# Regrouping the attention work inside the steps of a fused attention and feed-forward kernel, with exp(phi) one step sooner and q's transpose called at the front of its step

## The chip, the cores and the metric

The kernel runs on one core of one Trainium2 chip. The metric is the device time of one execution in microseconds (us). A profile's span, from its first to its last instruction, is about 1.8 us shorter than the time of the same execution.

## The reference, cut to what matters

Each of 8 batches pools k and v with weights made from phi, attends from q to the 32 pooled memories of each of 8 heads, and the result x goes through a normalised two-layer feed-forward with a residual:

```python
a = np.exp(phi - max); a = a / (np.sum(a, axis=2, keepdims=True) + 1e-09)
k_m = np.einsum('bhsm,bhsd->bhmd', a, k)
v_m = np.einsum('bhsm,bhsd->bhmd', a, v)
attn = softmax(scale * np.matmul(q, k_m.transpose(0, 1, 3, 2)))
x = np.matmul(attn, v_m)                       # then heads side by side: 8 x 576 x 512
xn = (x - mu) / np.sqrt(var + 1e-06) * g_ln
out = x + np.maximum(xn @ w_ch1, 0.0) @ w_ch2  # 512 -> 2048 -> 512
```

## The kernel before

The kernel works in steps, one for each batch b. A step has the first product of b (`mm1`, PSUM tiles h_ps), then the second product (`mm2`, ch_ps), four tiles of 128 rows in an even step and five in an odd one. Between the half tiles of the second product, 8 matmuls each, stands the attention work of the next batch, nb = b + 1, in the slots `ex[0]`, `ex[1]` and so on. Pooling is `a_kv`, the sums of the pooling weights `a_sum`, the transposes of the pooled k and v `a_tr`, the scores `a_sc`, the softmax's denominators `a_den` (which ends in Eh, the normalised weights), the first product's weights with v folded in `a_w1b`, and x and its statistics `x_tiles`.

```python
    for b in range(1, B):
        mm1(b, 0, JC)
        ...
        if b > 1:
            x_rstd(pr, tiles[0:2])
        if nb < B:
            ex[0] += [lambda: a_exp(nb), lambda: a_qT(nb, 0), lambda: a_kv(nb)]
            if nb + 1 < B:
                ex[0] += [lambda: phis.update({nb + 1: load_phi(nb + 1)})]
            ex[1] += [lambda: a_tr(nb)]
        ...
        ex[1] += [lambda: x_tiles(pr, t1)]
        if nb < B:
            ex[2] += [lambda: a_sum(nb), lambda: a_w1b(nb, 0), lambda: a_w1b(nb, 1)]
            ex[3] += [lambda: a_sc(nb)]
            ex[3] += [lambda: a_vb(nb)]
            ex[4] += [lambda: a_den(nb)]
            ex[5] += [lambda: a_w1b(nb, 2), lambda: a_w1b(nb, 3)]
            ex[6] += [lambda: x_tiles(nb // 2, [4, 5] if nb % 2 else [0, 1])]
            if nb + 1 < B:
                ex[7] += [lambda: load(nb + 1)]
```

`load` puts k, v and q of a batch into GpSimd's queue, which converts them to bf16 on the way; the pre-summation of exp(phi) for the sums (es) stands in the same queue, in program order. The transposed q comes from a DMA that the sync queue issues:

```python
    def a_qT(b, i):
        ...
                nc.sync.dma_start_transpose(out=s["qT"].rearrange("p j n x -> p (j n) x"),
                                            in_=s["q"].rearrange("p j n x -> p (j n x)"))
```

And nearly all PSUM tiles of the attention work rotate through one set of three buffers (`tag="big", bufs=3`).

The softmax here doesn't subtract the row's maximum and nothing guards it: scores larger than these inputs give would overflow.

## Time and profile before

| | before |
|---|---|
| time, median of 4 runs | 262.76 us |
| span of the profiled run | 261.1 us |
| TensorE busy | 245.4 us, 94% |
| granted TensorE clock, mean | 0.993 |
| second product, odd step (batch 3) | 22.63 us |
| second product, even step (batch 2) | 18.25 us |

The prediction below shows the lines that carry this. These are rows of the timeline of before in batch 2: start, length of the issue, instruction.

```profile
93.36 3.15 SPq L287 DMA_TRANSPOSE qT<-q_bf  x1
...
104.57 0.79 POOL L84 DMA_DIRECT2D kv_bf<-in_k_dram  x1
...
105.36 0.76 POOL L84 DMA_DIRECT2D kv_bf<-in_v_dram  x1
...
106.34 0.77 POOL L92 DMA_DIRECT2D q_bf<-in_q_dram  x1
...
107.93 0.47 PE L310 MATMUL sc_ps<-qT,kvT 64*32 64x320 bf16 x16
```

The transposing DMA of q is issued early in the first product, and lands 5.0 us later by the trace's list of DMA issues (median of six). The loads for the batch after next go out 11 us after it, when it is long done. They have to wait that long because GpSimd first works on es, and es waits for exp(phi), which stands behind the first product on ScalarE. Nobody wrote this order down as a rule: it is a by-product of where exp(phi) stands.

### The profile page before, as it was taken

The numbers are of one execution on the slowest core, as the hardware profiler recorded it, in microseconds if no ns is written. First come the engines' busy times: TensorE is split into PE (matmuls) and PEld (weight loads), VectorE is DVE, ScalarE is ACT, GpSimd is POOL, SyncE is SP. The second block draws the span as 40 slices with busy tenths as digits, with TensorE's granted clock in tenths as the row PEclk, the third lists the DMA queues.
The fourth block names the chain that finished last, engine by engine and source line by source line (L and its number), as shares of the span: only waits on it lengthen the run. The fifth ranks groups of instructions, "written<-read, shape, count | busy, mean of one in ns | idle before, by whom it ended". The sixth has DMA issues, their size and how long they took to land.

```text
span 261.1 us, 5808 instructions
## 1 busy us (share of the span) xinstructions
PE 245.4 (94%) x2453; PEld 132.2 (51%) x2453; DVE 154.9 (59%) x307; ACT 127.9 (49%) x218; POOL 51.9 (20%) x87
## 2 busy tenths in 40 slices
PE   7868996989989999999999999999999999999994
PEld 3434642437533475447543574457443664466453
DVE  3346716576485943876385754695477637684431
ACT  3165643356545185448546283647345472566210
POOL 8633230000440005400440007100710014000000
PEclk9999998999999999999999999999999999999999
DMA  7999999965689193895589391988499451121133
GB/s 159 195 207 207 206 253 251 244 138 102 134 118 234 43 182 92 153 233 114 128 143 210 81 199 56 189 186 120 137 182 189 90 94 43 44 55 25 43 80 80
DMA packets 41922, 36.82 MB, mean 141 GB/s; under 512 B 17444, under 2 KB 37160, under 8 KB 41896
## 3 DMA queue, kind: packets, MB, share of 16 engines
q0 software_dynamic: 17248, 19.53, 43.8%
q1 hardware_dynamic: 24488, 16.79, 28.0%
q8 instruction: 19, 0.31, 0.4%
q10 hardware_dynamic: 160, 0.13, 0.2%
q14 instruction: 7, 0.06, 0.1%
HBM read 41.42 MB, written 9.44 MB: 195 GB/s over the span
## 4 chain that ended last, share of the span: by engine, by line
PE 64%; DMA 18%; DVE 10%; ACT 4%; POOL 2%; issue 1%; SPq 0%; POOLq 0%
PE ch_ps L438 33%; PE h_ps L374 21%; DMA phi_st<-in_phi_dram 7%; DMA out_dram<-x_sb 6%; DMA w1r<-in_moe_w_ch_dram 4%; DVE w1b L357 3%; DVE bst L416 3%; PE kv_ps L205 2%; PE o_ps L404 2%; DVE Eh L339 2%; ACT x_sb L410 2%; PE w1b_ps L353 1%; PE last_ps L450 1%; DVE x_sb L462 1%; POOL kv_bf L84 1%
## 5 line engine op out<-in xcount | busy, mean ns | idle before, releaser
L438 PE MATMUL ch_ps<-w2b,rT 128*128 128x512 bf16 x560 | 131.8, 382 | 2.2 <-DVE x_sb L462 2.2
L438 PEld LDWEIGHTS <-rT 128*128 128x128 bf16 x560 | 51.2, 98 | 64.5 <-issue 9.6
L380 ACT ACTIVATE rT<-h_ps 128x576 bf16<-128x576 f32 x88 | 52.6, 649 | 33.0 <-PE h_ps L374 32.9
L374 PE MATMUL h_ps<-Eh,w1b 128*128 128x288 bf16 x512 | 67.3, 285 | 1.5 <-DVE w1b L357 0.8
L374 PEld LDWEIGHTS <-w1b 128*128 128x128 bf16 x512 | 49.5, 97 | 18.8 <-issue 2.7
L382 DVE TENSOR_SCALAR rT<-h_ps 128x576 bf16<-128x576 f32 x40 | 30.3, 756 | 26.9 <-PE h_ps L374 26.9
L357 DVE SCALAR_TENSOR_TENSOR w1b<-m_sb,rsum,w1b_ps 128x512 bf16<-128x512 f32 x64 | 43.6, 739 | 2.9 <-ACT m_sb L169 2.9
L189 POOL TENSOR_TENSOR es<-e_sb 128x512 f32<-128x512 bf16 x6 | 6.9, 1148 | 144.1 <-ACT e_sb L182 144.1
L462 DVE SCALAR_TENSOR_TENSOR x_sb<-ch_ps,rstd,x_sb 128x512 f32<-128x512 f32 x35 | 25.9, 742 | 13.2 <-PE ch_ps L438 12.6
L410 ACT ACTIVATE x_sb<-o_ps 128x1024 f32<-128x1024 f32 (+1 forms) x20 | 18.6, 937 | 29.5 <-PE o_ps L404 28.2
L416 DVE BATCH_NORM_STATS2 bst<-x_sb 128x6 f32<-128x512 f32 x36 | 24.4, 677 | 11.8 <-ACT x_sb L410 11.8
L339 DVE SCALAR_TENSOR_TENSOR Eh<-E_sb,rs,rden 128x576 bf16<-128x576 bf16 x16 | 12.4, 815 | 15.1 <-ACT rden L338 15.1
L315 ACT ACTIVATE E_sb<-sc_ps,rs 128x640 bf16<-128x640 f32 x16 | 11.9, 791 | 13.3 <-PE sc_ps L310 13.3
L424 ACT ACTIVATE rstd<-mv,eps_sb 128x2 f32<-128x2 f32 (+1 forms) x20 | 5.9, 296 | 20.3 <-DVE mv L417 20.3
L353 PE MATMUL w1b_ps<-w1r,kvT 64*32 64x512 bf16 x256 | 11.4, 383 | 1.3 <-DVE w1b L357 0.5
L182 ACT ACTIVATE e_sb<-phi_st 128x1152 bf16<-128x1152 f32 x8 | 9.2, 1153 | 6.2 <-DMA phi_st<-in_phi_dram 6.2
L227 DVE CAST v<-kv_ps 128x128 bf16<-128x128 f32 x8 | 2.3, 292 | 14.6 <-ACT k L220 13.7
L329 ACT ACTIVATE rden<-den_ps 128x576 f32<-128x576 f32 x16 | 9.5, 644 | 2.9 <-PE den_ps L327 2.9
L174 PE MATMUL w_ps<-fill 128*128 128x512 f32 x14 | 9.2, 774 | 1.6 <-DVE fill L119 1.6
L338 ACT ACTIVATE rden<-rden 128x576 f32<-128x576 f32 x16 | 10.0, 682 | 0.0
L404 PE MATMUL o_ps<-vb,Eh 64*128 64x128 bf16 (+1 forms) x160 | 8.5, 221 | 0.9 <-DVE Eh L339 0.9
L205 PEld LDWEIGHTS <-e_sb 64*32 64x32 bf16 x648 | 6.4, 94 | 5.4 <-ACT e_sb L182 3.0
(69 smaller groups left out, 143.4 us busy)
## 6 DMA issues: line engine op xcount, KB each, us to landing
out_dram<-x_sb SPq DMA_DIRECT2D x70, 128.0 KB, 2.4
kv_bf<-in_k_dram POOLq DMA_DIRECT2D x7, 576.0 KB, 6.4
kv_bf<-in_v_dram POOLq DMA_DIRECT2D x7, 576.0 KB, 9.1
phi_st<-in_phi_dram SPq DMA_DIRECT2D x6, 576.0 KB, 4.6
q_bf<-in_q_dram POOLq DMA_DIRECT2D x6, 576.0 KB, 11.7
w1r<-in_moe_w_ch_dram POOLq DMA_DIRECT2D x4, 512.0 KB, 14.2
w2b<-in_moe_w_ch_dram POOLq DMA_DIRECT2D x4, 512.0 KB, 19.3
q_bf<-in_q_dram POOLq DMA_DIRECT2D x4, 288.0 KB, 11.9
```

The lines of the kernel that those rows point to most:

```text
L315: nc.scalar.activation(out=E_[:, g].rearrange("p (a x) -> p a x", a=2), in_=sc[:, :, 0:HP], func=AF.Exp, scale=s["rs"][:, g:g + 1])
L339: nc.vector.scalar_tensor_tensor(out=Eh[:, g, :], in0=s["E"][:, g, 0:S], scalar=s["rs"][:, g:g + 1], in1=rd[:, g].rearrange("p a x -> p (a ...
L353: nc.tensor.matmul(ps[32 * j:32 * (j + 1), g, :], s["kvT"][r:r + 64, 2, 32 * j:32 * (j + 1)], w1r[r:r + 64, j, fs], start=True, stop=True, ...
L357: nc.vector.scalar_tensor_tensor(out=s["w1b"][:, g, fs], in0=m_sb[:, fs], scalar=s["rsum"][:, g:g + 1], in1=ps[:, g, :], op0=ALU.mult, op1 ...
L374: nc.tensor.matmul(h_ps[:, half, 0:HS], s["w1b"][:, g, P * j:P * (j + 1)], s["Eh"][:, g, HS * half:HS * (half + 1)], start=(g == 0), stop= ...
L380: nc.scalar.activation(out=dst, in_=h_ps[:, :, 0:HS], func=AF.Relu)
L382: nc.vector.tensor_scalar(out=dst, in0=h_ps[:, :, 0:HS], scalar1=0.0, scalar2=None, op0=ALU.max)
L404: nc.tensor.matmul(ov.rearrange("p (j e d) -> p j e d", e=2, d=D)[:, :, g, :], s["Eh"][r:r + 64, g, a:z], s["vb"][r:r + 64, g, 2 * u:2 * ( ...
L410: nc.scalar.activation(out=x[:, 0:n].rearrange("p i (u y) -> p i u y", u=2), in_=o_ps.rearrange("p u (i y) -> p i u y", i=2)[:, 0:n], func ...
L416: nc.vector.bn_stats(out=stt, in_=x[:, i, :])
L438: nc.tensor.matmul(ch_ps, rT[:, j, P * t:P * (t + 1)], w2b[:, j, :], start=(j == 0), stop=(j == JC - 1))
L462: nc.vector.scalar_tensor_tensor(out=x, in0=ch_ps, scalar=rstd, in1=x, op0=ALU.mult, op1=ALU.add)
```

## The change

Its intent is to enter and leave the small tiled matmuls less often. Pooling, sums, x of all four full tiles and the transposes become one group after the first half tile; the scores follow one half tile later, all of w1b comes behind den. To have it all ready, exp(phi) moves to the end of the step before, and the call of q's transpose to the front of the step. The loads move in program order too, from `ex[7]` to `ex[2]`. The core of the diff, cuts marked:

```diff
     def a_kv(b):
         ...
+        else:
+            a_sum(b, ps)                # sums into kv's own PSUM tile
         k_out(b, ps, True)
         v_out(b, ps[:, :, D:2 * D])
 ...
-    a_exp(1)
     x_tiles(0, [0, 1])
     x_tiles(0, [2, 3])
 ...
     x_rstd(0, [2, 3])
+    a_exp(1)
 ...
     load(2)
+    a_exp(2)
     for b in range(1, B):
+        if nb < B:
+            a_qT(nb, 0)
         mm1(b, 0, JC)
 ...
-            ex[0] += [lambda: a_exp(nb), lambda: a_qT(nb, 0), lambda: a_kv(nb)]
 ...
+            ex[0] += [lambda: a_kv(nb)]
 ...
+        ex[0] += [lambda: x_tiles(pr, t0, False), lambda: x_tiles(pr, t1, False)]
+            ex[0] += [lambda: a_tr(nb)]
 ...
+        ex[0] += [lambda: x_stats(pr, t0), lambda: x_rstd(pr, t0)]
+            ex[1] += [lambda: a_sc(nb)]
 ...
+        ex[1] += [lambda: x_stats(pr, t1), lambda: x_rstd(pr, t1)]
 ...
+            ex[3] += [lambda: x_tiles(pr, t2), lambda: x_rstd(pr, t2)]     # odd steps
 ...
+            ex[3] += [lambda: a_den(nb)]
+            ex[4] += [lambda: a_w1b(nb, 0), lambda: a_w1b(nb, 1), lambda: a_vb(nb)]
             ex[5] += [lambda: a_w1b(nb, 2), lambda: a_w1b(nb, 3)]
 ...
-                ex[7] += [lambda: load(nb + 1)]
 ...
+            ex[1] += [lambda: phis.update({nb + 1: load_phi(nb + 1)})]
+            ex[2] += [lambda: load(nb + 1)]
+            ex[6] += [lambda: a_exp(nb + 1)]
```

More of the change, by code (lines that the diff above doesn't have):

```diff
@@ L233, in rs_out, with a_sum @@
         st8[b]["rs"] = rs
+    def a_sum(b, ps):
+        for i in range(2):
+            nc.tensor.matmul(ps[:, 0, P:P + 2], st8[b]["es"][:, i, :], ones8,
+                             start=(i == 0), stop=(i == 1))
+        rs_out(b, ps)
     def a_kv(b):
@@ L263, in a_tr @@
             s["rsum"] = rsum
-    def a_sum(b):
-        ps = big([P, 2, 512], FP32, "sum_ps")
-        for i in range(2):
-            nc.tensor.matmul(ps[:, 0, P:P + 2], st8[b]["es"][:, i, :], ones8,
-                             start=(i == 0), stop=(i == 1))
-        rs_out(b, ps)
     def a_vb(b):
@@ L296, in a_qT @@
         dst = s["qT"][:, 2 * i:2 * i + 2].rearrange("p a n x -> p a (n x)")
-        if i == 0:
+        if i == 0 or b == 1:
             nc.scalar.activation(out=dst, in_=q_ps[:, :, 0:NP * P], func=AF.Copy)
@@ L385, with x_tiles @@
     xs = {}
-    def x_tiles(pr, ts):
+    def x_tiles(pr, ts, stats=True):
         n = len(ts)
@@ L412, in x_tiles, with x_stats @@
                              func=AF.Copy)
+        for i, t in enumerate(ts):
+            xs[(pr, t)] = (x, i)
+        if stats:
+            x_stats(pr, ts)
+    def x_stats(pr, ts):
+        x, n = xs[(pr, ts[0])][0], len(ts)
         mv = moe.tile([P, 2, 2], FP32, name="mv", bufs=4)
@@ L536 @@
     a_qT(1, 0)
+    a_w1b(1, 0)
     mm2(0, 2, 8, 12)
     a_qT(1, 1)
-    a_w1b(1, 0)
+    a_w1b(1, 1)
     mm2(0, 2, 12, 16)
     a_sc(1)
-    a_w1b(1, 1)
     mm2(0, 3, 0, 4)
     a_den(1)
-    a_vb(1)
     a_w1b(1, 2)
@@ L548 @@
     a_w1b(1, 3)
+    a_vb(1)
     mm2(0, 3, 8, 16)
     load(2)
+    a_exp(2)
     for b in range(1, B):
         pr = b // 2
-        mm1(b, 0, JC)
+        nb = b + 1
         odd = b % 2
         tiles = [4, 5, 6, 7, 8] if odd else [0, 1, 2, 3]
-        t1, t2 = tiles[2:4], tiles[4:5]
-        nb = b + 1
-        if b > 1:
-            x_rstd(pr, tiles[0:2])
+        t0, t1, t2 = tiles[0:2], tiles[2:4], tiles[4:5]
+        if nb < B:
+            a_qT(nb, 0)
+        mm1(b, 0, JC)
         ex = {i: [] for i in range(2 * len(tiles))}
         if nb < B:
-            ex[0] += [lambda: a_exp(nb), lambda: a_qT(nb, 0), lambda: a_kv(nb)]
-            if nb + 1 < B:
-                ex[0] += [lambda: phis.update({nb + 1: load_phi(nb + 1)})]
-            ex[1] += [lambda: a_tr(nb)]
-        if b == 1:
-            ex[0] += [lambda: x_tiles(0, [4, 5]), lambda: x_rstd(0, [4, 5])]
-        ex[1] += [lambda: x_tiles(pr, t1)]
+            ex[0] += [lambda: a_kv(nb)]
+        ex[0] += [lambda: x_tiles(pr, t0, False), lambda: x_tiles(pr, t1, False)]
         if nb < B:
-            ex[2] += [lambda: a_sum(nb), lambda: a_w1b(nb, 0), lambda: a_w1b(nb, 1)]
-        ex[2] += [lambda: x_rstd(pr, t1)]
+            ex[0] += [lambda: a_tr(nb)]
+        ex[0] += [lambda: x_stats(pr, t0), lambda: x_rstd(pr, t0)]
         if nb < B:
-            ex[3] += [lambda: a_sc(nb)]
+            ex[1] += [lambda: a_sc(nb)]
+        ex[1] += [lambda: x_stats(pr, t1), lambda: x_rstd(pr, t1)]
         if odd:
-            ex[4] += [lambda: x_tiles(pr, t2), lambda: x_rstd(pr, t2)]
+            ex[3] += [lambda: x_tiles(pr, t2), lambda: x_rstd(pr, t2)]
         if nb < B:
-            ex[3] += [lambda: a_vb(nb)]
-            ex[4] += [lambda: a_den(nb)]
+            ex[3] += [lambda: a_den(nb)]
+            ex[4] += [lambda: a_w1b(nb, 0), lambda: a_w1b(nb, 1), lambda: a_vb(nb)]
             ex[5] += [lambda: a_w1b(nb, 2), lambda: a_w1b(nb, 3)]
-            ex[6] += [lambda: x_tiles(nb // 2, [4, 5] if nb % 2 else [0, 1])]
-            if nb + 1 < B:
-                ex[7] += [lambda: load(nb + 1)]
+        if nb + 1 < B:
+            ex[1] += [lambda: phis.update({nb + 1: load_phi(nb + 1)})]
+            ex[2] += [lambda: load(nb + 1)]
+            ex[6] += [lambda: a_exp(nb + 1)]
         for i, t in enumerate(tiles):
```

## The prediction

> **What bounds the kernel now.** I read the page first, then the chain of waits in order of time, then the timelines of the prologue and of one pair of batch steps.
>
> ```profile
> span 261.1 us, 5808 instructions
> PE 245.4 (94%) x2453; PEld 132.2 (51%) x2453; DVE 154.9 (59%) x307; ACT 127.9 (49%) x218; POOL 51.9 (20%) x87
> PE   7868996989989999999999999999999999999994
> ```
>
> TensorE is the bound: from slice 16 to 39 every slice is at 90% or more, and no other engine is above 59%. So only three things move the end: matmul work on TensorE, the cost of changing between kinds of matmul, and stalls of TensorE. The chain of waits shows one even step (four tiles), columns being start, length, what:
>
> ```profile
> 98.87 1.73 PE ch_ps L438 x8
> 100.62 0.80 PE kv_ps L205 x72
> 101.42 1.83 PE ch_ps L438 x8
> ...
> 112.44 0.56 PE w1b_ps L353 x16
> 113.00 1.83 PE ch_ps L438 x8
> 114.83 0.46 PE o_ps L404 x12
> ```
>
> Eight matmuls of the second product take 1.73 us after full-array work and 1.83 after the 64-row attention matmuls: leaving a tiled group costs 0.10. Entering costs about as much: x of one pair of full tiles is four slots of 0.053 but takes 0.33. An inserted tiled group therefore costs about 0.22 beyond its work. By the stretches' table an even step's second product is 18.25 us (98.87 to 117.12) and an odd one's 22.63 (125.26 to 147.89), against 8 x 1.73 = 13.84 and 10 x 1.73 = 17.30; the first product adds 7.95 to 8.14. An even step has almost no stall. An odd one has about 0.8: the second product of batch 3, where the lines are start, length, instruction, and in brackets idle time and its releaser:
>
> ```profile
> 138.88 1.17 ACT L329 ACTIVATE rden<-den_ps 128x576 f32<-128x576 f32 x2
> 139.57 0.11 PEld L353 LDWEIGHTS <-kvT 64*32 64x32 bf16 x7 [0.37 <-issue]
> 140.66 1.55 DVE L339 SCALAR_TENSOR_TENSOR Eh<-E_sb,rs,rden 128x576 bf16<-128x576 bf16 x2 [2.25 <-ACT rden L338]
> 142.79 2.71 DVE L357 SCALAR_TENSOR_TENSOR w1b<-m_sb,rsum,w1b_ps 128x512 bf16<-128x512 f32 x4
> ```
>
> The second w1b group sat 0.3 us until Ln freed its PSUM buffer (three buffers rotate); and its evictions, 0.68 each, run only after both Eh operations, because VectorE keeps program order. The third place is the prologue:
>
> ```profile
> 37.14 1.16 ACT L182 ACTIVATE e_sb<-phi_st 128x1152 bf16<-128x1152 f32 x1 [3.58 <-DMA phi_st<-in_phi_dram]
> 38.21 1.92 ACT L410 ACTIVATE x_sb<-o_ps 128x1024 f32<-128x1024 f32 x2
> 43.24 1.87 PE L438 MATMUL ch_ps<-w2b,rT 128*128 128x512 bf16 x4 [2.21 <-DVE x_sb L462]
> 46.56 0.17 DVE L232 RECIPROCAL rs<-kv_ps 128x2 f32<-128x2 f32 x1 [2.72 <-PE kv_ps L213]
> 46.77 0.38 ACT L220 ACTIVATE k<-kv_ps 128x256 bf16<-128x256 f32 x1 [3.67 <-DVE rs L232]
> 47.18 0.29 DVE L227 CAST v<-kv_ps 128x128 bf16<-128x128 f32 x1 [0.45 <-ACT k L220]
> ```
>
> exp(phi 1) blocks ScalarE until phi has landed, so the x copies are late, and TensorE stands 2.21 us. The last three lines: reciprocal, k and v read one PSUM tile one after another.
>
> **What the Trainium skill says.** "TensorEngine Tiling (Array Packing)", Key Properties: changing the tiling mode drains TensorE. The 1.83 against 1.73 agrees. "PSUM — Partial Sum Buffer", Terms: two engines may not be on one bank at once, reads included. The trace agrees in effect: k waits for rs and v for k. "Perfetto Trace Analysis", Tensor Engine Instruction: ScalarE and VectorE are strict FIFO; Eh before w1b above agrees. "DMA: Bandwidth & Descriptors", Issuing engines are not separate DMA queues: transfers of all queues interleave on the same 16 engines; the prologue's outputs will slow its loads.
>
> **The change part by part.** No arithmetic goes away except that sums no longer take a PSUM tile of their own; nearly everything is moved.
>
> *Prologue.* exp(phi 1) goes behind the rstd pair. The x copies can then start at the end of x, about 33.9, instead of 38.21; statistics end near 38.3, rstd near 38.8, exp(phi 1) near 40.0. The 2.21 us stall goes, and pooling could start at about 41.8 instead of 45.0. But v of batch 1 is issued at 23.08 and takes 19.5 to landing: 42.6. And two outputs of 128 KB now leave before that; at the 206 GB/s shown there they take some 1.3 us of the loads. I put pooling at 43.7, a gain of 1.4. Afterwards the order to the first product of batch 1 is much as before (Eh about 10.3 us after pooling starts, w1b evictions behind it, the first product waiting for them). The two qT copies, 1.24 us on ScalarE each, overlap mm2. **-1.4 us.**
>
> *The group at the front of each step.* After half a tile (1.75 us from the start of the second product): kv 0.80, sums about 0.1, x of two pairs 0.55 (even) or 0.68 (odd), transposes 0.2. But before the transposes come rs (0.04 + 0.14), k (to 0.63 after the sums) and v (to 0.95 after), from the spacing of the three lines above. x covers 0.55 to 0.68 of that, and the transposes' PSUM buffer is kv's own in a rotation of three (kv, x, x, then again), so they wait for v's copy: 0.3 to 0.45 us of stall. The group takes 2.15. Before, the same parts took kv 0.80 + 0.10, transposes 0.17, x 0.33 + 0.46 with their switches, sums 0.03: 2.1. So the switch saved (0.22) is paid back by the new wait. **0.**
>
> *Statistics.* They now fall inside the step. x copies end 4.3 and 5.3 us after the second product's start, statistics of the first pair at 6.3, rstd 6.9, first output 7.6. The accumulators have two buffers; the third tile asks at about 10. No stall.
>
> *Scores, den, w1b.* Scores at 5.6, exp of scores to 8.4, den at 9.6. Both w1b pairs now come right behind den, in two successive half tiles, where before the first pair stood three half tiles ahead of den. **Even step:** den from 9.6; Eh ends 3.63 after den's start (from 110.23 and 112.31 + 1.55 in the trace): 13.2. First pair's matmuls 11.8 to 12.4, its evictions 13.2 to 15.9. The second pair is asked for at 14.2; its second group needs the buffer of the first pair's first, free at 14.6: 0.1 stall. Then vb 0.5, an output 0.7 and four evictions keep VectorE to 19.7, while the next first product starts at 18.45: its third PSUM buffer comes 0.3 late (0.18 was lost there before). Sum with the small differences **+0.3**. **Odd step:** x of the ninth tile, its statistics and rstd stand ahead of Ln, so Eh ends 5.67 after that x begins (136.54 to 142.21 in the trace): 9.6 + 5.67 = 15.3. w1b's first pair 12.0 to 12.9, with the same 0.3 stall as now. The second pair is asked for at 14.7, its second group at 15.0, and its buffer is that of the first group, whose two evictions (1.35) start at 15.3: free at 16.65. **TensorE stands 1.6 us.** The step's second product is then 17.0 + 4 x 1.73 + 0.1 = 24.0 against 22.63: **+1.4** in batches 3 and 5. In batch 1 the present one is 24.12 (it has extra stalls and an extra x): **-0.1**.
>
> *Last step.* It takes over x of its first pair: **+0.4**.
>
> *Loads and exp(phi) sooner.* GpSimd's sums finish long before the pooling that needs them, and exp is off the path between activations. The exp of before cost TensorE nearly nothing in the steady steps (kv starts 0.02 after the half tile). The transposing DMA stands behind the same outputs in its queue, so it starts about where it does now. **0.**
>
> Sum: -1.4 - 0.1 + 2 x 1.4 + 3 x 0.3 + 0.4 = **+2.6**, or 265.2 us.
>
> **The rivals.**
>
> (a) The merge pays as meant: two PSUM rotations or a slightly earlier Eh make the w1b wait vanish, and one switch per step is saved. For it: every odd step now loses 0.8, part of it TensorE waiting for Eh in front of x of the next batch (0.5), which goes. Then odd steps gain 0.5 each, the prologue 1.4 to 2.4, and the time would be near 259.5. Against it: the rotation of three is what the stall at 139.57 shows, and VectorE's order is fixed.
>
> (b) VectorE becomes the bound in the second half of even steps too. It has to do Eh 1.55, eight evictions 5.4, vb 0.5 and two outputs 1.5, about 9 us, in the 7 us between den's result and the next first product. The overflow stalls the first product's PSUM buffers; I count 0.3, but it could be 1.0 three times: 267.5. Against it: the first product's first evictions are ScalarE's.
>
> (c) The prologue alone decides: v, q and outputs share the DMA engines, and the qT transposes (q's last part lands at 45.5 now) wait. Then the -1.4 shrinks to nothing: 266.6.
>
> **Range and chances.** Worked sum 265.2; I give rival (a) a quarter and stay a little below the sum: **264.3 us**, range **259.5 to 267.6**. 2% is 257.4 below and 267.9 above. Faster by over 2% needs all of (a) and a full prologue gain: 0.07. Slower needs (b) with the odd stall: 0.09. Within 2%: 0.84.
>
> **What would show it.** Right: the wait of the second product for the x_sb output near 43 is gone, pooling of batch 1 starts between 42.6 and 44.5; in odd steps w1b_ps matmuls wait on VectorE's w1b by 1 to 2 us; the kvT_ps transposes wait 0.3 to 0.5 on v's copy in every step; the second product stretches of batches 3 and 5 are near 24.0. Wrong: odd stretches at or below 22.6 with no w1b wait (rival a); even steps' h_ps waiting on w1b by 1 us (rival b); pooling of batch 1 at 45 (rival c).

## The result, and the profile after

The changed kernel takes 280.45 us (median of 4 runs, 278.9 to 281.16), against 262.76 before: slower, ratio 1.0665, 95% interval 1.0609 to 1.0721. A ratio here and below is the mean time of one kernel's fast runs over that of the other's fast runs of the same rounds, so it is not quite the ratio of the medians. Executions over 1.5% slower than the fastest of the same kernel are left out of the means. The prediction was 264.3 in a range of 259.5 to 267.6.

The page of the changed kernel has the same matmul work and lower shares:

```profile
span 279.2 us, 5784 instructions
PE 245.7 (88%) x2421; PEld 132.9 (48%) x2453; DVE 156.4 (56%) x306; ACT 128.3 (46%) x219; POOL 53.0 (19%) x87
...
PE   7769998989297999999597999999497999999994
...
PEclk9999999999779999999999999999979999999998
...
PE 51%; DMA 21%; DVE 15%; ACT 7%; issue 3%; POOL 1%; SPq 1%; DVEq 0%; POOLq 0%
```

TensorE's busy time is 245.7 us against 245.4, but 32 matmul records are missing here (2421 of 2453), so it reads too low. The same kernel's trace in the last control run has all of them: 247.7 us busy in a span of 279.8. There, of 18.7 us more span, 16.4 are time in which TensorE stands and 2.3 are more busy time. Its row of slices has three holes (a 2, a 5 and a 4) that the row of before has not, and the clock row has dips to 7 behind the first and the last of them. The table of waits (engine, line, what it waited for: total us, times, longest) names them:

```profile
PE sc_ps L311 <- DMA qT<-q_bf: 11.1, 3, 5.2
...
PE w1b_ps L354 <- DVE w1b L358: 4.3, 3, 1.4
...
PE kvT_ps L260 <- DVE v L227: 2.9, 6, 0.5
```

The second and third were predicted, nearly with their sizes (1.43 us where 1.6 was put, 0.41 to 0.54 where 0.3 to 0.45 was put). The first was not: in each odd step the scores wait for the transposed q. The chain of waits (start, length, what) shows why in one place, batch 1:

```profile
57.38 0.63 POOL es L193
...
58.93 0.46 POOL kv_bf L84
...
59.69 15.62 DMA qT<-q_bf
...
75.44 0.73 PE sc_ps L311 x13
76.18 5.30 PE ch_ps L446 x16
```

The transposing DMA takes 15.62 us here. By the two traces' lists of DMA issues, its median time to landing was 5.0 us before (first line) and is 12.2 now (second):

```profile
qT<-q_bf SPq DMA_TRANSPOSE x6, 5.0
...
qT<-q_bf SPq DMA_TRANSPOSE x6, 12.2
```

In batch 1 it is issued where it always was, 4.5 us after the first product began (before: 4.6). But 0.8 us before it GpSimd issued the load of k for the batch after next, and those of v and q follow at 59.72 and 60.70: es is done at 58.9 now because exp(phi) came a step sooner, and the loads go out right behind it. Before, in this step, the load of k left at 72.08, and the transpose was issued at 61.98. In batch 6, behind which there is nothing left to load, the transposing DMA takes 5.0 us in the changed kernel too. In batches 2 and 4 it is slowed as well (9.6 and 10.9 us), but it lands before the scores' turn (in batch 2 at about 107.6, the scores start at 109.49), so only the odd steps wait.

The table of stretches has the second products of batches 1, 2, 3 and 5. Its columns are the stretch, its length, the busy time of PE, PEld, DVE, ACT and POOL with instruction counts, the granted clock, the share of DMA and GB/s:

```profile
64.54:95.70 31.16, 23.87 (x229) 10.34 (x232) 15.88 (x32) 9.12 (x18) 6.21 (x10) 0.89 0.65 117
103.87:122.32 18.45, 17.70 (x205) 8.14 (x208) 13.20 (x28) 8.26 (x15) 3.86 (x7) 1.00 0.43 104
130.87:157.58 26.71, 21.87 (x230) 9.88 (x233) 15.88 (x32) 9.12 (x18) 6.22 (x10) 1.00 0.67 117
192.98:221.93 28.95, 23.77 (x229) 10.41 (x232) 15.88 (x32) 9.12 (x18) 3.68 (x6) 0.94 0.54 99
```

The odd ones are 31.16, 26.71 and 28.95 us where 24.0 was predicted; the even one is 18.45. (This trace lacks the record of each second product's first matmul, so these read some 0.2 us short, and the first products as much long.) In batches 1 and 5 the clock is below 1: after the waits of 5.21 and 3.11 us the next sixteen matmuls took 5.3 us instead of 3.6.

### The profile page after: what moved, and what is told of

It is laid out like the page before. It is cut to its first block, busy times and chain, and to the rows that moved or that the text cites. A ratio compares the mean times of both kernels' runs of the same rounds, so it can differ in the third digit from the quotient of the medians.

```text
span 279.2 us, 5784 instructions
## 1 busy us (share of the span) xinstructions
PE 245.7 (88%) x2421; PEld 132.9 (48%) x2453; DVE 156.4 (56%) x306; ACT 128.3 (46%) x219; POOL 53.0 (19%) x87
## 3 DMA queue, kind: packets, MB, share of 16 engines
HBM read 41.42 MB, written 9.44 MB: 182 GB/s over the span
## 4 chain that ended last, share of the span: by engine, by line
PE 51%; DMA 21%; DVE 15%; ACT 7%; issue 3%; POOL 1%; SPq 1%; DVEq 0%; POOLq 0%
PE ch_ps L446 28%; PE h_ps L375 16%; DMA qT<-q_bf 11%; DVE w1b L358 8%; DMA w1r<-in_moe_w_ch_dram 5%; ACT rden L330 2%; DMA q_bf<-in_q_dram 2%; DVE Eh L340 2%; DVE x_sb L470 1%; ACT rden L339 1%; DMA phi_st<-in_phi_dram 1%; PE kv_ps L205 1%; PE last_ps L458 1%; DVE bst L424 1%; PE sc_ps L311 1%
## 5 line engine op out<-in xcount | busy, mean ns | idle before, releaser
L446 PE MATMUL ch_ps<-w2b,rT 128*128 128x512 bf16 x530 | 128.0, 387 | 1.5
L446 PEld LDWEIGHTS <-rT 128*128 128x128 bf16 x560 | 53.2, 99 | 65.0 <-issue 10.9
L381 ACT ACTIVATE rT<-h_ps 128x576 bf16<-128x576 f32 x88 | 52.9, 649 | 58.9 <-PE h_ps L375 58.6
L358 DVE SCALAR_TENSOR_TENSOR w1b<-m_sb,rsum,w1b_ps 128x512 bf16<-128x512 f32 x64 | 43.7, 741 | 3.5 <-ACT m_sb L169 2.7
L411 ACT ACTIVATE x_sb<-o_ps 128x1024 f32<-128x1024 f32 (+1 forms) x20 | 17.9, 938 | 11.7 <-PE o_ps L405 9.7
L354 PE MATMUL w1b_ps<-w1r,kvT 64*32 64x512 bf16 x256 | 12.5, 385 | 4.7 <-DVE w1b L358 4.3
L311 PE MATMUL sc_ps<-qT,kvT 64*32 64x320 bf16 x128 | 4.3, 320 | 11.6 <-DMA qT<-q_bf 11.1
L220 ACT ACTIVATE k<-kv_ps 128x256 bf16<-128x256 f32 x7 | 2.7, 384 | 20.2 <-DVE rs L232 20.2
L354 PEld LDWEIGHTS <-kvT 64*32 64x32 bf16 x256 | 3.3, 88 | 15.0 <-issue 8.1
```

The source lines that it names most:

```text
L354: nc.tensor.matmul(ps[32 * j:32 * (j + 1), g, :], s["kvT"][r:r + 64, 2, 32 * j:32 * (j + 1)], w1r[r:r + 64, j, fs], start=True, stop=True, ...
L358: nc.vector.scalar_tensor_tensor(out=s["w1b"][:, g, fs], in0=m_sb[:, fs], scalar=s["rsum"][:, g:g + 1], in1=ps[:, g, :], op0=ALU.mult, op1 ...
L381: nc.scalar.activation(out=dst, in_=h_ps[:, :, 0:HS], func=AF.Relu)
L411: nc.scalar.activation(out=x[:, 0:n].rearrange("p i (u y) -> p i u y", u=2), in_=o_ps.rearrange("p u (i y) -> p i u y", i=2)[:, 0:n], func ...
L446: nc.tensor.matmul(ch_ps, rT[:, j, P * t:P * (t + 1)], w2b[:, j, :], start=(j == 0), stop=(j == JC - 1))
```

## The experiments

The theory after this reading: (T) the early loads make the transposing DMA slow, and the scores, which now come early, wait for it; the full loss needs both. What is left is what the prediction had worked out. The rivals: moving the scores forward does it whatever the loads do; the waits for w1b or something on GpSimd or ScalarE is the larger part; the dropped clock is a loss of its own.

### The loads held back

```diff
+    def load(b, after=None):
+        if after is not None:
+            hold = att.tile([P, 2], BF16, name="hold")
+            nc.gpsimd.tensor_copy(out=hold, in_=after)
 ...
-            ex[2] += [lambda: load(nb + 1)]
+            ex[2] += [lambda: load(nb + 1, st8[nb]["rsum"])]
```

A tiny copy on GpSimd, of the v sums that VectorE makes behind the transposes' evictions, makes the loads wait for that point of the step; all else is the changed kernel.

> The changed kernel, but the loads of k, v and q for the batch after next are held back on GpSimd until the v sums of the present step are there (some 4.6 us into the second product), so that they no longer run beside the transposing DMA of q. Theory (the slow transposing DMA is the loads' doing, and the scores wait for it): the transposing DMA takes 5 us in every step instead of 10 to 15, the scores' 11 us of waits on qT vanish, the granted clock goes back to about 0.993, the time is about 265.5 us (264 to 267). Rival 1 (moving the scores forward alone makes the wait, whatever the loads do): waits of 2 us or more in each odd step stay, above 272. Rival 2 (w1b behind Eh is the main loss): unchanged, about 280. The wait of the fourth w1b group on VectorE, 1.43 us in odd steps, should stay in every case.

Measured: 265.95 us, ratio 1.0162 to the kernel before (1.0119 to 1.0205), clock 0.998. In batch 1, where the trace of the changed kernel has 15.62 us:

```profile
58.74 3.37 SPq L291 DMA_TRANSPOSE qT<-q_bf  x1
...
68.33 0.19 POOL L99 CAST hold<-rsum 128x2 bf16<-128x2 f32 x1 [10.41 <-DVE rsum L274]
...
68.85 0.78 POOL L84 DMA_DIRECT2D kv_bf<-in_k_dram  x1 [0.34 <-issue]
...
69.20 0.47 PE L314 MATMUL sc_ps<-qT,kvT 64*32 64x320 bf16 x16
```

The loads go out 10 us after the transpose, which takes a median of 5.0 us (6.2 in this batch); the scores, as early as in the changed kernel, wait for nothing. Exp and sums are a step sooner here too. So it is the loads, and the first two rivals fall.

### The scores read an old q

```diff
+            if i == 0:
+                s["qT_new"] = att.tile([P, 4, NP, P], BF16, name="qT")
+                nc.sync.dma_start_transpose(out=s["qT_new"].rearrange("p j n x -> p (j n) x"),
+                                            in_=s["q"].rearrange("p j n x -> p (j n x)"))
+                s["qT"] = st8[1]["qT"]
+            return
 ...
-            s["qT"] = att.tile([P, 4, NP, P], BF16, name="qT")
+            s["qT"] = (consts if b == 1 else att).tile([P, 4, NP, P], BF16, name="qT1" if b == 1 else "qT")
```

The DMA still fills its tile, but the scores read batch 1's, which is kept in a tile of its own. This computes with the wrong q. (It still came within the comparison's tolerance, so that comparison says nothing about the scores.)

> Wrong result on purpose: the changed kernel with all its loads and transposing DMAs where they are, but the scores read batch 1's transposed q from a tile of its own, so nothing waits for the transposing DMA. Theory: the DMA still takes 10 to 15 us in most steps, the scores do not wait, the time is about 265.5 us (264 to 267), the same as with the loads held back. Rival (the early loads also slow something else, SBUF traffic or the outputs): clearly above 268.

Measured: 265.84 us, ratio 1.0142 (1.0097 to 1.0188). The trace's list of DMA issues has the transposing DMA at a median of 12.3 us, as slow as in the changed kernel; nothing waits for it. The slow transfer itself costs nothing, the wait for it does, and the early loads harm nothing else that shows. This run also shows the change without its accident, stretch by stretch (batches 1, 2, 3):

```profile
64.64:88.72 24.08, 22.17 (x235) 9.93 (x233) 15.90 (x32) 9.32 (x18) 6.21 (x10) 1.00 0.86 150
96.69:115.35 18.66, 18.07 (x212) 8.24 (x210) 13.21 (x27) 8.45 (x15) 3.72 (x7) 1.00 0.45 105
123.82:147.91 24.09, 22.18 (x236) 9.97 (x234) 15.90 (x32) 9.33 (x18) 6.22 (x10) 1.00 0.67 130
```

### exp(phi) sooner alone, in the kernel before

```diff
-            ex[0] += [lambda: a_exp(nb), lambda: a_qT(nb, 0), lambda: a_kv(nb)]
+            ex[0] += [lambda: a_qT(nb, 0), lambda: a_kv(nb)]
 ...
-                ex[7] += [lambda: load(nb + 1)]
+                ex[7] += [lambda: load(nb + 1), lambda: a_exp(nb + 1)]
```

> The kernel before with one part of the change alone: exp(phi) one step sooner, at the end of the step before, which lets GpSimd issue the loads one step sooner too. Scores stay where they were, four half tiles into the second product. Theory: the transposing DMA lengthens to 10 to 15 us here too, but as the scores come 3.6 us later than in the changed kernel, most of it stays hidden: waits of 0 to 1.5 us per odd step, 262.5 to 266 us. Rival (exp and sums sooner cost in themselves, through GpSimd and VectorE sharing or ScalarE): above 268 with the transposing DMA at 5 us.

Measured: 263.75 us, ratio 1.0076 (1.0037 to 1.0115). The transposing DMA's median is 12.5 us: exp(phi) sooner alone starts the collision, with the loads still at `ex[7]`. The scores stand two half tiles later here, and most of it stays hidden:

```profile
PE sc_ps L310 <- DMA qT<-q_bf: 2.7, 3, 1.4
```

With the two runs above this closes the square of waits for q: 2.7 us with early loads alone (0.8% in the time), none with the scores forward and the loads held back, 11.1 us with both.

### Idle matmuls ahead of the scores

```diff
             sc = big([P, 2, 512], FP32, "sc_ps")
+            if g == 0 and b in (2, 4, 6):
+                for _ in range(12):
+                    nc.tensor.matmul(sc[:, 0, :], w2b[:, 0, 0:P], w2b[:, 0, :], start=True, stop=True)
```

> The changed kernel with 12 idle matmuls of 128x512 (2.6 us) ahead of the scores in the odd steps, where TensorE waits 2.8 to 5.2 us for qT; the scores overwrite their result. Theory (part of the loss is the clock that drops after the wait): the wait for qT becomes 0.2 to 2.6 us, the sixteen matmuls behind it take 3.5 us instead of 5.3 in batches 1 and 5, the mean granted clock rises from 0.98 to about 0.993, the time falls by about 3.7 us to some 276.7. Rival (the clock has nothing to do with the idle TensorE): no change or slower, 280 to 282.

Measured: 279.27 us, ratio 1.0668 (1.0617 to 1.072), clock 0.992. The profiled execution had the clock up and the sixteen matmuls behind the wait in batch 1 at 3.63 us, but the time did not follow. As its chip was not that of the changed kernel's run, both were run together:

> The changed kernel as a control on the same chip as the next run: ratio 1.066 to 1.076, granted clock about 0.98, the sixteen matmuls behind the longest waits for qT take 5.3 us.

> The kernel with 12 idle matmuls ahead of the scores in odd steps, again, beside the changed kernel. Its first run had the clock at 0.992 and the sixteen matmuls at 3.6 us, but its ratio, 1.0668, was that of the changed kernel on another chip. Theory A (the dropped clock is a loss of its own): 2 to 4 us less than the control. Theory B (what the clock gives is taken again, since the transposing DMA ends with the loads and the next wait is longer): within 1 us of the control.

Measured: the control 280.5 us, ratio 1.0682 (1.0646 to 1.0718), clocks of its runs 0.979 to 0.988; with the idle matmuls 280.79 us, ratio 1.0722 (1.068 to 1.0764), clocks 0.985 to 0.994. So filling the wait gains nothing that shows in the time, though it raises the clock. I had expected 3.7 us. Why it is given back is only partly seen: the scores still start when the transposing DMA lands (75.05 us in batch 1, against 74.59 in the control), and in batch 1 of this execution the matmuls behind the wait took 5.26 us all the same. How much of the 14.6 us between 280.45 and 265.84 (13.7 by the two ratios, as the runs are of different rounds) belongs to the clock therefore stays open; that it goes away together with the waits is shown by the two runs above.

### The prologue's part alone, in the kernel before

```diff
-    a_exp(1)
     x_tiles(0, [0, 1])
 ...
     x_rstd(0, [2, 3])
+    a_exp(1)
     mm2(0, 0, 4, 16)
```

> The kernel before with one part of the change alone: exp(phi) of batch 1 behind the first two rstd pairs. Theory: the x copies start near 34 us instead of 38.2, the 2.2 us wait of the second product for its first output goes, the steps after it stay as they were (second products 22.63 and 18.25 us), so about 2.0 us less, 259.9 us (the changed kernel and the one with the old qT reached the second product of batch 1 2.0 us sooner). Rival (the gain is taken by the loads that it then waits for, k, v and q of batch 1): 0 to 1 us less.

Measured: 260.5 us, ratio 0.9929 (0.9898 to 0.996) on 262.03: by the ratio 1.9 us less, with an interval of 1.0 to 2.7 (the medians are 1.5 apart). The prologue's gain is real and stands by itself.

### w1b's first pair ahead of den again

On top of the held loads:

```diff
-            ex[3] += [lambda: a_den(nb)]
-            ex[4] += [lambda: a_w1b(nb, 0), lambda: a_w1b(nb, 1), lambda: a_vb(nb)]
-            ex[5] += [lambda: a_w1b(nb, 2), lambda: a_w1b(nb, 3)]
+            ex[2] += [lambda: a_w1b(nb, 0), lambda: a_w1b(nb, 1)]
+            ex[3 + odd] += [lambda: a_den(nb)]
+            ex[4 + odd] += [lambda: a_vb(nb)]
+            ex[5 + odd] += [lambda: a_w1b(nb, 2), lambda: a_w1b(nb, 3)]
```

> The changed kernel with held loads, and the first two w1b pairs back in front of den (third half tile), den and the last two pairs one half tile later in odd steps. Theory (what is left of the loss is w1b standing behind Eh on VectorE, and the buffers that wait for it): the waits of w1b_ps on VectorE (1.43 us in odd steps) and of h_ps behind even steps vanish, odd second products fall from 24.09 to about 22.0 us and even ones from 18.66 to about 18.3, 257.5 to 259.5 us, faster than the kernel before. Rival (the group at the front, its transposes' wait and one x more are the rest of the loss): odd stretches stay above 23 us, 263 us or more.

Measured: 261.13 us, ratio 0.9959 (0.9928 to 0.9989). The waits of w1b_ps on VectorE are gone and the odd second products are 21.97 us, as expected. The time is 1.6 to 3.6 us above what I had expected, and the timeline of the first product of batch 3 tells why:

```profile
114.29 1.16 ACT L185 ACTIVATE e_sb<-phi_st 128x1152 bf16<-128x1152 f32 x1 [6.94 <-DMA phi_st<-in_phi_dram]
115.36 1.71 ACT L384 ACTIVATE rT<-h_ps 128x576 bf16<-128x576 f32 x3
...
116.04 1.19 PE L378 MATMUL h_ps<-Eh,w1b 128*128 128x288 bf16 x8 [1.55 <-ACT rT L384]
```

The held loads run beside the load of phi, whose median time to landing is 10.5 us here against 4.2 in the changed kernel; exp waits 6.94 us for it at the head of ScalarE's queue, the first product's evictions stand behind exp, and TensorE behind them. (The run with the loads held back has this wait too: 6.70 us in the same place.) It is the same kind of accident, one transfer further on.

### phi ahead, and the reciprocal behind k and v

```diff
-            ex[1] += [lambda: phis.update({nb + 1: load_phi(nb + 1)})]
+            ex[0] += [lambda: phis.update({nb + 1: load_phi(nb + 1)})]
 ...
-        rs_out(b, ps)          # at the end of a_sum
+        if b >= 2:             # at the end of a_kv, behind k_out and v_out
+            rs_out(b, ps)
```

> As the run with w1b apart, and two small things more: the reciprocal of the sums reads the PSUM tile after k and v instead of before them, and phi is loaded ahead of the step's first output. Theory: the transposes' wait on v's copy (0.41 us in odd, 0.54 in even steps) falls by about 0.2 us in each of six steps, and the exp that waited up to 6.8 us for phi in even steps no longer holds up the next first product: 1 to 1.5 us less than with w1b apart alone, some 257 us. Rival (those waits lie beside other work): no change.

Measured: 257.52 us (257.05 to 257.89), ratio 0.9823 to the kernel before (0.9795 to 0.9851), correct. It is faster than both kernels. Batches 1, 2 and 3:

```profile
64.46:86.31 21.85, 21.30 (x229) 9.67 (x232) 16.07 (x32) 9.23 (x18) 6.32 (x11) 1.00 0.75 152
94.48:112.78 18.30, 17.68 (x205) 7.97 (x208) 14.14 (x29) 8.20 (x15) 6.38 (x11) 1.00 0.79 164
120.96:142.81 21.85, 21.30 (x230) 9.68 (x233) 16.07 (x32) 9.21 (x18) 6.32 (x11) 1.00 0.69 137
```

The steps of batches 2 and 3 take 56.50 us together (86.31 to 142.81, from first product to first product) against 56.97 before (90.76 to 147.73), the second product of batch 1 takes 21.85 against 24.12, and it begins 2.2 us sooner. (This trace and the one of the run before it lack 32 matmul records, so their second products read some 0.2 us short.) Most of the 3.6 us that this version gains on the one before it is the phi wait: the first products of batches 3 and 5 took 9.95 and 9.44 us there and take 8.18 and 8.17 here. The reciprocal's share is at most 0.13 us a step, from the stretches of batches 1 to 3 (21.98 to 21.85, 18.43 to 18.30).

### The control of that round

> The changed kernel once more, on the same chip as the others, as a control: 280 us, ratio 1.067, granted clock about 0.98.

Measured: 282.12 us, the median of three fast runs (280.11 to 283.94; a fourth, 284.61, was slow), ratio 1.0759 (1.0697 to 1.0821), clock 0.979 in the profiled run. It reads a little slower than the first time and the last, but the intervals overlap.

## Why the prediction was right or wrong

The outcome was outside the range, and one step made it so. It is the last of the working, "Loads and exp(phi) sooner": "The transposing DMA stands behind the same outputs in its queue, so it starts about where it does now. **0.**" The start was right, to 0.1 us in batch 1. The step asked where the transfer starts and not what would run beside it. It had the parts in hand: exp(phi) sooner lets GpSimd's es finish sooner, and the loads stand behind es in the same queue. In its place the runs showed 9.6 to 15.6 us for the transfer while there was something to load, 11.1 us of waits for it, and with the slower matmuls behind them 14.6 us in the three odd steps (31.16, 26.71 and 28.95 in the changed kernel against 24.08, 24.09 and 24.09 with the old q). The worked sum was +2.6 us, given as 265.2 (on the median of 262.76 it would be 265.4). Without this one wait the kernel takes 265.84, which is 3.7 us more than before by the ratio. That 265.2 and 265.84 lie so close is partly luck: the runs of before in that round were at 261.88, and the even steps' term was too small.

The other steps, in their order:

- *Prologue, -1.4.* Right in mechanism; whether it was too small isn't clear. Pooling of batch 1 started at 43.28 us (43.7 predicted) and the second product of batch 1 at 64.54 instead of 66.64, 2.1 us sooner (single traces of other runs with the same prologue differ: 63.36 with the loads held, 64.64 with the old q); alone it is worth 1.9 us, interval 1.0 to 2.7.
- *The group, 0, with a new wait of 0.3 to 0.45 us in front of the transposes.* The wait was there: 0.41 us on v's copy in odd steps, 0.54 in even ones, a little above the range. That the sum is 0 was not measured by itself.
- *Statistics, 0.* Right: no accumulator was late.
- *w1b behind Eh, odd steps, a stall of 1.6 us and a second product of 24.0.* Right: 1.43 us three times, and 24.08 and 24.09 where the transposed q does not intrude.
- *w1b, even steps, +0.3.* The wait of the first product on w1b was sized right: 0.34 and 0.43 us in batches 3 and 5 with the old q, and 8.47 and 8.56 us for these first products against 8.13. The sum was too small, as the even second products grew too, 18.66 against 18.25: 0.8 together in batches 2 and 4. The second w1b pair stands about 0.25 longer there (0.87 for its matmuls against 0.62, where 0.1 was put); the rest isn't taken apart.
- *Last step, +0.4.* Right: 22.41 against 22.03.

Of the rivals, (a), that the w1b wait vanishes, fell: the wait was there. (b), VectorE as the bound in even steps, was there at 0.4 us instead of the 1.0 that would have been needed. (c), loads and outputs sharing the DMA engines, had the right actors in the wrong place: it looked at the prologue, where it cost little, and not at the steps.

## What to carry to other kernels

When an operation moves to an earlier place, follow what stands behind it in every queue: transfers that a late operation used to hold back will start with it, and may run beside one that the critical path is about to wait for. Check for each transfer not only when it starts but what else is on the DMA engines until it lands, and if the order matters, say so in the program (a small copy that waits for the right moment was enough here) rather than leave it to an accident. A change that fails by such an accident may still hold good parts: with two transfers put in order and w1b set apart, this one ended 1.8% faster than the kernel before.

## What the Trainium skill lacked or had wrong

- "DMA: Bandwidth & Descriptors": its section on DMA Transpose gives constraints, and a table further up has an effective bandwidth of 261 GB/s for such a DMA on one kernel, but neither has a time for one that runs beside other transfers. Here one transfer of q takes 5.0 us in the median of before (5.0 to 6.5), and 9.6 to 15.6 us beside three loads of 576 KB in the changed kernel.
- "TensorE: Matmul & The Clock Gate", HAM oscillation: its rule for real kernels is to have no idle gaps of more than about 3.4 us. This case agrees in the direction, but the edge is not sharp: in three profiles of the changed kernel the clock fell behind waits of 5.21, 5.16, 5.03 and 3.96 us and also behind 3.11 and 3.21, not behind 2.76 and 2.79, nor behind one of 3.42. With the idle matmuls just ahead of the wait it fell behind 2.75 us in one profile and not behind 3.14 in another. What the page does not lead one to expect: keeping TensorE busy through part of the wait raised the mean clock from about 0.98 to 0.99 and gained no time (ratio 1.0722 against 1.0682).
- No page has the cost of a reader added in front of others on one PSUM tile: with the reciprocal in front of k and v the transposes waited 0.41 to 0.54 us, with it behind them 0.28 to 0.41 us.
